# Segment 0 of a memory-recurrent attention during the weight loads, with V stores on two queues and part of chunk 1 projected early

## The chip, the core and the metric

One core of a Trainium2 chip runs the kernel. The metric is the time of one execution on the device in microseconds (us); for the kernel before it is the median of eight runs. A profile is one execution taken by the hardware profiler; its span runs from the first to the last instruction.

The engines are PE (TensorE: matmuls, with weight loads shown as PEld), DVE (VectorE), ACT (ScalarE), POOL (GpSimd) and SP (SyncE, which only issues DMAs here). Sixteen DMA engines move data for queues that SP, ACT and POOL feed.

## The reference, cut to what matters

```python
h  = x + A(layernorm(x), mem0, Wq, Wk, Wv, Wo)     # x: 2048 x 512
out = h + B(layernorm(h), w_in, w_sp, b_sp, w_out)

def A(x, mem, ...):                # 32 heads of 128, 64 segments of 32 rows, 8 memory rows
    for s in range(64):
        hs = concat([mem, x[32*s:32*s+32]])           # 40 rows
        q, k, v = hs @ Wq, hs @ Wk, hs @ Wv           # 512 -> 32 heads x 128
        p = softmax(mask(q @ k.T * scale))
        o = (p @ v) @ Wo                              # back to 512
        mem = o[:8]; outs.append(o[8:])               # the next segment needs this one's memory
def B(x, ...):                     # a gated MLP with a 2048 x 2048 mixing of the rows
    z = gelu(x @ w_in); z1, z2 = split(z); z2 = layernorm(z2)
    return (z1 * (w_sp @ z2 + b_sp)) @ w_out
```

Part A is a recurrence of 64 segments: the memory rows that a segment puts out go into the next one.

## The kernel before, in words

A small emitter records every operation in program order with the tiles that it reads and writes; each engine then executes its own operations in that order, with semaphore waits where another engine's result is needed (`Emitter.add`, L57). A DMA is an operation of the queue that issues it: SP for nearly all. DMAs take one of 40 semaphores in turn.

**Load phase.** SP loads two tiles of x, then Wq, Wk, Wv and Wo, each in four pieces of 1 MB (L287, L703). Of the 32 rows of a segment, the last 8 ("extra rows", the segment length less the memory rows gives 24 others) are projected to Q, K and V ahead of time, 16 segments (a *chunk*) at once: a tile hTe holds the 128 extra rows of a chunk, transposed. `qkx_mm` (L371) is one group of 16 matmuls, four heads of Q or K; `qkx_evac` (L383) moves it to QTx. `vx_mm` (L392) is one group for V; `vx_evac` (L401) moves it to one of two Vs buffers and a DMA stores that to vext_d in DRAM, from which `load_vx` (L412) fetches what a segment needs into Vx. In the load phase chunk 0 is done: 16 Q/K groups (L690) and 8 V groups (L705 to L708), whose stores are issued by ACT. `ln_inplace` (L331) normalises a tile of x (DVE and POOL in turn), `xT` (L342) transposes it on PE, `ring_copy` and `xe_copy` move it to hT (24 rows of each of four segments) and hTe (extra rows). `late_consts` (L303) makes masks and selectors on POOL.

**Segment loop** (L764). A segment does in order: Q and K for two halves of the heads (`QK`, L431; PE L437), eviction and transposition (`QK_evac`, ACT and DVE), scores (`S_half`), exp, V (`V_half`, L531), sums, reciprocal and normalisation of the softmax, p times v (`PV_half`, L548 and L554, the latter with Vx), eviction to cT, `Wo` (L581), eviction to part (one of eight slots), `mem_out` (L600 and L603), which writes the next segment's memory rows to hT. Between these PE gets other work by hand: `gx.pour(16)` (L819) puts one Q/K group of the next chunk ahead of `PV_half`; `gv.pour` puts the four pieces (four matmuls each) of a V group at L833 (one, ahead of Wo), L847 (two, after Wo) and L856 (one, after mem_out), in the segments whose index in the chunk is in VXS (L745). So chunk c is projected while chunk c-1 runs, and in segments 48 to 63 nothing is poured. Every fourth segment adds the four segments' results to x (`F_group`, `h_done`). Every second segment SP transposes a piece of w_sp by DMA (`wT_piece`, L778).

After segment 63 part B runs; it is not touched.

Of the kernel before, what the change touches and what calls it, by code (L numbers as in the profile page):

```python
# [33 lines left out]
class Emitter:  # L34
    ENGS = ("pe", "act", "dve", "pool", "sp")

    def __init__(self, n_dma_sems=16):
        self.ops = []
        self.by_eng = {e: [] for e in self.ENGS}
        self.last_w = {}  # L40
        self.readers = {}
        self.n_dma_sems = n_dma_sems
        self.dma_rr = 0
        self.dma_cnt = [0] * n_dma_sems
        self.dma_last = [None] * n_dma_sems
        self.const_tokens = set()
# [4 lines left out]
    def add(self, eng, fn, reads=(), writes=(), dma=False, after=()):  # L51
# [17 lines left out]
        if eng == "pool" and self.by_eng["pool"]:  # L69
            deps.add(self.by_eng["pool"][-1])  # L70
        if eng == "pe":
            deps = {d for d in deps if d.eng != "pe" or d.is_dma}
        if dma:
            j = self.dma_rr
            self.dma_rr = (self.dma_rr + 1) % self.n_dma_sems
            op.is_dma = True
            op.dma_sem = j
            self.dma_cnt[j] += 1
            op.dma_val = 16 * self.dma_cnt[j]
            if self.dma_last[j] is not None:  # L80
                deps.add(self.dma_last[j])
            self.dma_last[j] = op
# [9 lines left out]
        self.ops.append(op)  # L92
        op.pos = len(self.by_eng[eng])
# [67 lines left out]
def fast_path(nc, st, keep, A_x, A_mem0, A_Wq, A_Wk, A_Wv, A_Wo, A_seg_len, B_w_in, B_w_sp, B_b_sp, B_w_out, out):  # L161
# [15 lines left out]
    CK = 16  # L177
# [29 lines left out]
    hTe = sb("hTe", [128, 2, DC, 128], BF)  # L207
# [69 lines left out]
    def load_x(rb, j):  # L277
        sp(lambda e: e.dma_start(xn[:, j, :], xr[:, rb, :]), writes=[("xn", j)])

    def load_xe(ck, j):  # L280
        sp(lambda e: e.dma_start(xn[:, j, :], xe[CK * ck:CK * ck + CK, XM:SEG, :]), writes=[("xn", j)])
# [9 lines left out]
    load_xe(1, 1)  # L291
    for hq in range(4):
        load_w(0, hq)
    sp(lambda e: e.dma_start(m0[:], A_mem0[0]), writes=["m0"])
# [36 lines left out]
    def ln_inplace(j):  # L331
        dve(lambda e: e.bn_stats(out=st1[:, j, :], in_=xn[:, j, :]), reads=[("xn", j)], writes=[("st1", j)])
        dve(lambda e: e.bn_aggr(out=mv1[:, j, :], in_=st1[:, j, :]), reads=[("st1", j)], writes=[("mv1", j)])
        pool(lambda e: e.tensor_scalar(out=rs1[:, j:j + 1], in0=mv1[:, j, 1:2], scalar1=EPS, scalar2=None, op0=ALU.add),
             reads=[("mv1", j)], writes=[("rs1", j)])
        pool(lambda e: e.tensor_tensor(out=rs1[:, j:j + 1], in0=rs1[:, j:j + 1], in1=mhalf[:, 0:1], op=ALU.pow),
             reads=[("rs1", j), "mhalf"], writes=[("rs1", j)])
        dve(lambda e: e.tensor_scalar(out=xn[:, j, :], in0=xn[:, j, :], scalar1=mv1[:, j, 0:1], scalar2=rs1[:, j:j + 1],
                                      op0=ALU.subtract, op1=ALU.mult),
            reads=[("xn", j), ("mv1", j), ("rs1", j)], writes=[("xn", j)])  # L340

    def xT(j, bank):  # L342
        for dc in range(DC):
            pe(lambda e, dc=dc: e.transpose(out=psb[:, bank, dc * 128:(dc + 1) * 128], in_=xn[:, j, dc * 128:(dc + 1) * 128],
                                            identity=ident[:, :]),
               reads=[("xn", j), "ident"], writes=[PB(bank)])
# [10 lines left out]
    def xe_copy(ck, bank):  # L357
        src = psb[:, bank, 0:512].rearrange("p (dc c) -> p dc c", dc=DC)
        act(lambda e: e.activation(out=hTe[:, ck % 2, :, :], in_=src, func=ACT.Copy), reads=[PB(bank)], writes=[("hTe", ck % 2)])
# [10 lines left out]
    def qkx_mm(ck, i, bank, only_hh=None, only_dc=None):  # L370
        mi, h0 = i // 8, 4 * (i % 8)  # L371
        ws = (w_q, w_k)[mi]
        for hh in range(4):
            h = h0 + hh
            for dc in range(DC):
                if only_hh is not None and (hh, dc) != (only_hh, only_dc):
                    continue
                pe(lambda e, h=h, dc=dc, hh=hh: e.matmul(ps[:, bank, hh * 128:(hh + 1) * 128], lhsT=ws[:, dc, h * DH:(h + 1) * DH],  # L378
                                                         rhs=hTe[:, ck % 2, dc, :], start=(dc == 0), stop=(dc == DC - 1)),
                   reads=[("hTe", ck % 2), ("W", mi, h // 8)], writes=[PB(bank)])  # L380
# [10 lines left out]
    def vx_mm(ck, n, bank, only=None):  # L391
        for dc in range(DC):  # L392
            if only is not None and dc != only:
                continue
            for c in range(4):
                q = slice(32 * c, 32 * c + 32)
                pe(lambda e, dc=dc, c=c, q=q: e.matmul(ps[q, bank, :], lhsT=hTe[:, ck % 2, dc, q], rhs=w_v[:, dc, n * 512:(n + 1) * 512],  # L397
                                                       start=(dc == 0), stop=(dc == DC - 1), tile_position=(0, 32 * c)),
                   reads=[("hTe", ck % 2), ("W", 2, n // 2)], writes=[PB(bank)])

    def vx_evac(ck, n, bank, eng="act", queue="sp"):  # L401
        j = n % 2
        if eng == "act":
            act(lambda e: e.activation(out=Vs[:, j, :], in_=ps[:, bank, :], func=ACT.Copy), reads=[PB(bank)], writes=[("Vs", j)])
        else:
            dve(lambda e: e.tensor_copy(out=Vs[:, j, :], in_=ps[:, bank, :]), reads=[PB(bank)], writes=[("Vs", j)])
        b, c = n // 4, n % 4
        dst = vext_d[ck, 4 * c:4 * c + 4, :, b * DH:(b + 1) * DH].rearrange("g t e -> t g e")
        em.add(queue, lambda e: e.dma_start(dst, Vs[:, j, :].rearrange("p (g e) -> p g e", g=4)), dma=True, reads=[("Vs", j)],
               writes=[("vext", ck, n)])  # L410

    def load_vx(s):  # L412
        i = s % CK
        sp(lambda e: e.dma_start(Vx[:, s % NVX, :, :], vext_d[s // CK, :, 8 * i:8 * i + 8, :]),
           reads=[("vext", s // CK, n) for n in range(8)], writes=[("Vx", s % NVX)])
# [259 lines left out]
    for j in range(2):  # L675
        ln_inplace(j)
        xT(j, 6 + j)
        xe_copy(j, 6 + j)
    load_x(0, 0)
    load_x(1, 1)  # L680
    for hq in range(4):
        load_w(1, hq)
    late_consts()
    ebank = (0, 1, 2, 3)

    def start_group(cnt, mm, ev, *a):
        bk = ebank[cnt % 4]
        mm(*a, bk)
        ev(*a, bk, "act" if cnt % 2 == 0 else "dve")

    for i in range(16):
        start_group(i, qkx_mm, qkx_evac, 0, i)
        if i == 7:
            for j in range(2):
                ln_inplace(j)
                xT(j, 6 + j)
                ring_copy(j, 6 + j)
            mem0_transpose(5)
# [6 lines left out]
    for n in range(8):  # L705
        bk = ebank[n % 4]
        vx_mm(0, n, bk)
        vx_evac(0, n, bk, "act" if n % 2 == 0 else "dve", "act")  # L708
    for s in range(2):
        load_vx(s)  # L710
# [20 lines left out]
    gx, gv = Gap(), Gap()  # L731

    def qkx_atoms(ck, i):
        mms = [lambda ck=ck, i=i, hh=hh, dc=dc: qkx_mm(ck, i, XB, hh, dc) for hh in range(4) for dc in range(DC)]
        f = lambda: qkx_evac(ck, i, XB, "dve")
        f.eng = "dve"
        gx.add(XB, mms, f)

    def vx_atoms(ck, n):
        mms = [lambda ck=ck, n=n, dc=dc: vx_mm(ck, n, VXB, dc) for dc in range(DC)]  # L740
        f = lambda: vx_evac(ck, n, VXB, "act")
        f.eng = "act"
        gv.add(VXB, mms, f)

    VXS = (0, 1, 4, 5, 7, 8, 9, 12)  # L745
# [18 lines left out]
    for s in range(NSEG):  # L764
        j4 = s % 4
        rb = s // 4
        ck, i16 = s // CK + 1, s % CK
        if ck < NCK:
            if i16 == 0:
                for n in range(8):  # L770
                    vx_atoms(ck, n)
            qkx_atoms(ck, i16)
# [4 lines left out]
        if s % 2 == 0 and s // 2 < NWT:  # L777
# [3 lines left out]
        if i16 == 11 and 2 <= ck + 1 < NCK:  # L781
            load_xe(ck + 1, 1)
# [6 lines left out]
        if s == NSEG - 1:  # L789
            load_wT(0, [lastop["q"]])  # L790
        S_half(s, 0)
        sm_exp(0)
        V_half(s, 0)
# [11 lines left out]
        sm_rcp(0)  # L805
        V_half(s, 1, (0, 1, 2))
# [12 lines left out]
        ev = gx.pour(16)  # L819
# [12 lines left out]
        vx = i16 in VXS  # L832
        late = gv.pour(vx)  # L833
# [11 lines left out]
        if i16 == 12 and 2 <= ck + 1 < NCK:  # L845
            ln_inplace(1)
        late += gv.pour(2 * vx)  # L847
# [3 lines left out]
        if i16 == 13 and 2 <= ck + 1 < NCK:  # L851
            xT(1, XB)
            late.append(lambda: xe_copy(ck + 1, XB))
        if s + 1 < NSEG:
            mem_out(s)
        late += gv.pour(vx)  # L856
# [15 lines left out]
    assert not gx.atoms and not gv.atoms  # L872
# [922 lines left out]
```

## Time and profile before

| what | value |
|---|---|
| median of 8 runs | 941.97 us (939.97 to 944.39) |
| the profiled execution's own time | 940.55 us |
| its span | 938.7 us |
| PE busy | 881.3 us (94%) |
| ACT, DVE, POOL busy | 478.5, 445.3, 109.0 us |
| HBM read, written | 39.46 MB, 18.61 MB |
| first Q/K group (L378) on PE | 8.44 us |
| first V group (L397) on PE | 33.37 us |
| segment 0's Q and K (L437) | 49.92 us |
| segment 1's Q and K | 64.05 us |
| segment 48's Q and K | 582.49 us |

In the views a row begins with the line of the kernel, the engine and the operation; then the tile written and the tiles read, their shapes, and how many. A bracket at the end of a timeline row says how long the engine sat idle before it and what ended that. In the windows each row is a stretch of time: its length, the busy time of PE, PEld, DVE, ACT and POOL with the number of instructions, the granted clock of PE as a share of full speed, the busy share of the DMA engines and GB/s. In the chain of waits a row is a start, a duration and what the end of the program can be followed back to.

### The profile page before, as it was taken

To read this page: it belongs to the slowest core of one execution; us is meant where nothing else is said; L and a number is where in the kernel's file an instruction comes from. 1 tells how busy PE (TensorE), PEld (TensorE's weight loads), DVE (VectorE), ACT (ScalarE), POOL (GpSimd) and SP (SyncE) were. 2 spreads that over 40 slices of the span, in tenths; PEclk is the share of its full clock that TensorE was granted. 3 is DMA by queue.
4 is the path that set the end of the run, shared out by engine and by line. 5 is a ranking of instruction groups with operands and counts; after the bars stand their busy time and mean duration, and the time that the engine had idled before them with its cause. 6 is when DMAs were issued, how large, how long until landed. Compare 5 with 4: busy or idle time off the path is not lost.

```text
span 938.7 us, 45489 instructions
## 1 busy us (share of the span) xinstructions
PE 881.3 (94%) x20973; PEld 492.1 (52%) x20973; DVE 445.3 (47%) x1029; ACT 478.5 (51%) x1158; POOL 109.0 (12%) x274
## 2 busy tenths in 40 slices
PE   4789999999999999999999999989989999989998
PEld 4545555555555556555555555444544444434443
DVE  3134445455555445554545555444434464453434
ACT  2156566666666666666666656565656565500000
POOL 5001011011111111111111011111101022200000
PEclk9889999999999999999999999999999999999999
DMA  9942012130222222121212130513112193021201
GB/s 332 377 121 68 17 37 66 48 82 21 62 55 57 46 63 46 46 59 39 60 37 66 42 82 13 123 29 79 48 42 58 33 293 116 1 90 37 93 17 36
DMA packets 103668, 71.29 MB, mean 76 GB/s; under 512 B 62248, under 2 KB 89008, under 8 KB 103472
## 3 DMA queue, kind: packets, MB, share of 16 engines
q1 hardware_dynamic: 99248, 67.27, 24.9%
q8 instruction: 166, 2.72, 1.3%
q10 hardware_dynamic: 4224, 1.05, 0.5%
q14 instruction: 30, 0.25, 0.1%
HBM read 39.46 MB, written 18.61 MB: 62 GB/s over the span
## 4 chain that ended last, share of the span: by engine, by line
PE 89%; ACT 3%; DMA 3%; DVE 2%; issue 1%; SPq 0%; POOL 0%; ACTq 0%; DVEq 0%; POOLq 0%
PE f_ps L437 24%; PE f_ps L581 12%; PE f_ps L531 11%; PE f_ps L938 10%; PE f_ps L378 6%; PE f_ps L625 4%; PE f_ps L900 3%; PE f_ps L548 3%; PE f_ps L931 2%; PE f_ps L1008 2%; PE f_ps L397 2%; PE f_ps L600 2%; DMA vext_d<-f_Vs 2%; PE f_ps L476 2%; PE f_ps L497 1%
## 5 line engine op out<-in xcount | busy, mean ns | idle before, releaser
L437 PE MATMUL f_ps<-f_arena,f_hT 128*32 128x512 bf16 x4096 | 235.7, 383 | 17.9 <-ACT f_hT L603 12.0
L444 ACT ACTIVATE f_Tst<-f_ps 128x512 bf16<-128x512 f32 x256 | 152.6, 597 | 103.1 <-PE f_ps L437 101.2
L437 PEld LDWEIGHTS f_ps<-f_arena,f_hT 128*32 128x32 bf16 x4096 | 105.7, 97 | 127.4 <-ACT f_hT L603 24.0
L531 PE MATMUL f_ps<-f_arena,f_hT 128*32 128x512 bf16 x2048 | 140.2, 378 | 0.0
L450 DVE STREAM_TRANSPOSE f_QT<-f_Tst 128x256 uint32<-128x256 uint32 x128 | 57.0, 445 | 174.6 <-ACT f_Tst L444 174.6
L581 PE MATMUL f_ps<-f_arena,f_cT 128*32 128x384 bf16 (+1 forms) x4096 | 123.6, 273 | 1.6 <-ACT f_cT L567 1.5
L581 PEld LDWEIGHTS f_ps<-f_arena,f_cT 128*32 128x32 bf16 x4096 | 84.8, 97 | 55.4 <-ACT f_cT L567 26.4
L938 PE MATMUL f_ps<-f_arena 128*128 128x512 bf16 x448 | 101.3, 379 | 2.4 <-DVE f_arena L944 1.6
L593 ACT ACTIVATE f_part<-f_ps 128x384 bf16<-128x384 f32 (+1 forms) x128 | 46.4, 384 | 74.7 <-PE f_ps L581 74.7
L453 DVE STREAM_TRANSPOSE f_KT<-f_Tst 128x256 uint32<-128x256 uint32 x128 | 57.0, 445 | 52.7 <-ACT f_Tst L444 52.7
L460 POOL COPY f_QT<-f_arena 128x256 bf16<-128x256 bf16 x64 | 30.7, 480 | 392.2 <-PE f_ps L482 392.2
L569 DVE TENSOR_SCALAR f_cT<-f_ps 128x320 bf16<-128x320 f32 x128 | 56.9, 486 | 38.2 <-PE f_ps L554 38.2
L938 PEld LDWEIGHTS f_ps<-f_arena 128*128 128x128 bf16 x448 | 43.5, 98 | 55.9 <-DVE f_arena L944 2.6
L378 PE MATMUL f_ps<-f_hTe,f_arena 128*128 128x128 bf16 x1024 | 69.3, 225 | 0.7 <-DMA f_arena<-in_A_Wq_dram 0.7
L378 PEld LDWEIGHTS f_ps<-f_hTe,f_arena 128*128 128x128 bf16 x1024 | 60.7, 101 | 12.3 <-issue 12.3
L567 ACT ACTIVATE f_cT<-f_ps 128x320 bf16<-128x320 f32 x128 | 49.0, 435 | 34.2 <-PE f_ps L554 34.2
L517 DVE SCALAR_TENSOR_TENSOR f_E_sb<-f_R_sb,f_E_sb 128x160 bf16<-128x160 f32 x128 | 41.7, 326 | 46.5 <-ACT f_R_sb L513 46.5
L509 ACT ACTIVATE f_R_sb<-f_ps 128x160 f32<-128x160 f32 x128 | 39.0, 304 | 35.8 <-PE f_ps L502 35.8
L531 PEld LDWEIGHTS f_ps<-f_arena,f_hT 128*32 128x32 bf16 x2048 | 44.6, 95 | 21.0
L589 POOL COPY f_cTx<-f_cT 128x256 bf16<-128x256 bf16 x64 | 26.2, 410 | 196.6 <-DVE f_cT L569 196.6
L944 DVE TENSOR_TENSOR f_arena<-f_ps,f_arena 128x512 f32<-128x512 f32 x28 | 19.3, 691 | 57.8 <-PE f_ps L938 57.8
L389 DVE CAST f_arena<-f_ps 128x512 bf16<-128x512 f32 x56 | 38.2, 683 | 16.0 <-PE f_ps L378 16.0
(95 smaller groups left out, 1086.9 us busy)
## 6 DMA issues: line engine op xcount, KB each, us to landing
wT_d<-f_wst SPq DMA_DIRECT2D x32, 256.0 KB, 2.5
f_arena<-wT_d SPq DMA_DIRECT2D x32, 256.0 KB, 4.3
f_arena<-in_A_Wq_dram SPq DMA_DIRECT2D x4, 1024.0 KB, 8.8
f_arena<-in_A_Wk_dram SPq DMA_DIRECT2D x4, 1024.0 KB, 14.0
f_arena<-in_A_Wv_dram SPq DMA_DIRECT2D x4, 1024.0 KB, 14.5
f_arena<-in_A_Wo_dram SPq DMA_DIRECT2D x4, 1024.0 KB, 15.3
f_Vx<-vext_d SPq DMA_DIRECT2D x64, 64.0 KB, 2.9
vext_d<-f_Vs SPq DMA_DIRECT2D x24, 128.0 KB, 2.1
```

Of the source, the lines that this page charges most:

```text
L378: pe(lambda e, h=h, dc=dc, hh=hh: e.matmul(ps[:, bank, hh * 128:(hh + 1) * 128], lhsT=ws[:, dc, h * DH:(h + 1) * DH], rhs=hTe[:, ck % 2, d ...
L437: pe(lambda e, dc=dc, c=c, rhs=rhs: e.matmul(ps[32 * c:32 * c + 32, bank, :], lhsT=hT[:, sl, dc, :], rhs=rhs, start=(dc == 0), stop=(dc == ...
L444: act(lambda e: e.activation(out=Tst[:, tb, :].rearrange("p (hp i r) -> p hp i r", i=32, r=2), in_=ps[:, bank, :].rearrange("p (hp r i) -> ...
L450: dve(lambda e: e.transpose(out=dst, in_=src), reads=[("T", tb)], writes=[("QT", b)])
L453: dve(lambda e: e.transpose(out=dst, in_=src), reads=[("T", tb)], writes=[("KT", b)])
L517: dve(lambda e: e.scalar_tensor_tensor(out=E_sb[:, b, 0:160], in0=R_sb[:, b, :], scalar=RK, in1=E_sb[:, b, 0:160], op0=ALU.mult, op1=ALU.m ...
L531: pe(lambda e, dc=dc, c=c, c0=c0: e.matmul(ps[32 * c:32 * c + 32, bank, :], lhsT=hT[:, sl, dc, :], rhs=w_v[:, dc, c0:c0 + 512], start=(dc ...
L567: act(lambda e: e.activation(out=dst, in_=src, func=ACT.Copy, scale=UNSC), reads=[PB(PVB[c])], writes=[("cT", c)])
L569: dve(lambda e: e.tensor_scalar(out=dst, in0=src, scalar1=UNSC, scalar2=None, op0=ALU.mult), reads=[PB(PVB[c])], writes=[("cT", c)])
L581: pe(lambda e, h=h, g=g, i=i, b=b, c=c: e.matmul(ps[32 * g:32 * g + 32, bank, 0:d1 - d0], lhsT=cTh[:, i, 8:40], rhs=w_o[:, h, d0:d1], star ...
L593: act(lambda e: e.activation(out=part[:, s % 8, d0:d1], in_=ps[:, bank, 0:d1 - d0], func=ACT.Copy), reads=[PB(bank)], writes=[("part", s % ...
L938: pe(lambda e: e.matmul(ps[:, bank, 0:TB], lhsT=z2[:, sc, fb * 128:(fb + 1) * 128], rhs=wTb[tb % 2][:, :, sc, :], start=(sc == 0), stop=(s ...
```

## The change

Eight things are done. (1) x tiles of the start are loaded into free slots of `part` as well, all ahead of Wk, and hTe has three buffers, so the extra rows of chunk 2 are prepared at the start; those of chunk 3 are loaded at segment 4. (2) The groups of the load phase rotate over banks 2 to 5, so that segment 0's Q and K (banks 0, 1, 6, 7) can follow directly. (3) The first four Q/K groups of chunk 1 are put between those of chunk 0. (4) The eight V groups of chunk 0 move into segment 0, two, two and four at a time. (5) They are evicted to the eight slots of `part`, so no eviction waits for an earlier store; the stores alternate between ACT's and POOL's queue; the first two Vx loads are issued by POOL; POOL's DMAs have four semaphores of their own and POOL's compute no longer takes a POOL DMA as its predecessor. (6) Q/K groups 4 to 7 of chunk 1 follow in segment 0. (7) In the segments the slot ahead of `PV_half` takes whole groups from one list: the 8 V groups of chunk 1, its remaining 8 Q/K groups, then those of chunks 2 and 3. The V pieces of chunks 2 and 3 are poured one after mem_out in every segment and one more after Wo in two of four. (8) `wT_piece` moves from even to odd segments, `late_consts` behind the four norms of the load phase.

```diff
@@ Emitter.add
-        if eng == "pool" and self.by_eng["pool"]:
-            deps.add(self.by_eng["pool"][-1])
+        if eng == "pool" and not dma:
+            if self.last_pool is not None:
+                deps.add(self.last_pool)
...
         if dma:
-            j = self.dma_rr
-            self.dma_rr = (self.dma_rr + 1) % self.n_dma_sems
+            if eng == "pool":
+                self.sw_rr = (self.sw_rr + 1) % 4
+                j = self.n_dma_sems - 4 + self.sw_rr
+            else:
+                j = self.dma_rr
+                self.dma_rr = (self.dma_rr + 1) % (self.n_dma_sems - 4)
...
-    hTe = sb("hTe", [128, 2, DC, 128], BF)
+    hTe = sb("hTe", [128, 3, DC, 128], BF)
...
+    def xbuf(j):
+        return (xn[:, j, :], [("xn", j)]) if j < 2 else (part[:, j, :], [("part", j, 0), ("part", j, 1)])
...
     load_xe(0, 0)
-    load_xe(1, 1)
     for hq in range(4):
         load_w(0, hq)
+    load_xe(1, 1)
+    load_x(0, 4)
+    load_x(1, 5)
+    load_xe(2, 6)
...
     def vx_evac(ck, n, bank, eng="act", queue="sp"):
-        j = n % 2
+        if ck == 0:
+            t, tok = part[:, n, :], [("part", n, 0), ("part", n, 1)]
+        else:
+            j = vcnt[0] % 2
+            vcnt[0] += 1
+            t, tok = Vs[:, j, :], [("Vs", j)]
...
-    def load_vx(s):
+    def load_vx(s, queue="sp"):
...
-    for j in range(2):
-        ln_inplace(j)
-        xT(j, 6 + j)
-        xe_copy(j, 6 + j)
-    load_x(0, 0)
-    load_x(1, 1)
+    ln_inplace(0)
+    xT(0, 6)
+    xe_copy(0, 6)
     for hq in range(4):
         load_w(1, hq)
-    late_consts()
-    ebank = (0, 1, 2, 3)
+    ebank = (2, 3, 4, 5)
...
+        if mm is vx_mm:
+            ev(*a, bk, eng, {"act": "act", "dve": "pool"}[eng])
...
     for i in range(16):
-        start_group(i, qkx_mm, qkx_evac, 0, i)
+        start_x(0, i)
+        if i == 5:
+            ln_inplace(1)
+            ln_inplace(4)
         if i == 7:
-            for j in range(2):
-                ln_inplace(j)
-                xT(j, 6 + j)
-                ring_copy(j, 6 + j)
-            mem0_transpose(5)
+            ln_inplace(5)
+            ln_inplace(6)
+            late_consts()
...
+        if i >= 9 and i % 2 == 1:
+            start_x(1, i // 2 - 4)
...
-    for n in range(8):
-        bk = ebank[n % 4]
-        vx_mm(0, n, bk)
-        vx_evac(0, n, bk, "act" if n % 2 == 0 else "dve", "act")
-    for s in range(2):
-        load_vx(s)
...
+    for n in range(8):
+        vx_group(1, n)
+    for ck, i0 in ((1, 8), (2, 0), (3, 0)):
+        for i in range(i0, 16):
+            qkx_group(ck, i)
+    for ck in (2, 3):
+        for n in range(8):
+            vx_atoms(ck, n)
...
-        if s % 2 == 0 and s // 2 < NWT:
+        if s % 2 == 1 and s // 2 < NWT:
             wT_piece(s // 2)
...
+        if s == 0:
+            for n in range(2):
+                start_v(n)
         S_half(s, 0)
         sm_exp(0)
+        if s == 0:
+            for n in range(2, 4):
+                start_v(n)
         V_half(s, 0)
...
+        if s == 0:
+            for n in range(4, 8):
+                start_v(n)
         V_half(s, 1, (0, 1, 2))
...
-        ev = gx.pour(16)
+        if s == 0:
+            for j in range(2):
+                load_vx(j, "pool")
+            for i in range(4, 8):
+                start_x(1, i)
+        ev = [gx.pop(0)()] if gx else []
         PV_half(s, 0)
...
-        late += gv.pour(2 * vx)
+        if j4 < 2:
+            late += gv.pour(1)
...
-        late += gv.pour(vx)
+        late += gv.pour(1)
```

## The prediction, made before the changed kernel ran

> **What bounds the kernel now.** I read the page first: PE is busy for 94% of a span of 938.7 us and holds 89% of the chain that ended last. That share is an average over stages, so I went to the two stages that the change touches: the loading of the weights, and the 64 segments.
>
> The start, by windows of 1 us (the last two columns are the share of the DMA engines and GB/s, before them the granted clock), then the chain of waits and the timeline over 0 to 65 us:
>
> ```profile
> 35.00:36.00 1.00, 1.00 (x28) 0.45 (x21) 0.66 (x1) 0.07 (x1) 0.00 (x0) 1.00 1.06 391
> 40.00:41.00 1.00, 0.00 (x0) 0.00 (x0) 0.00 (x0) 0.00 (x0) 0.00 (x0) 1.00 1.14 360
> 49.00:50.00 1.00, 0.08 (x4) 0.08 (x8) 0.00 (x0) 0.60 (x1) 0.00 (x0) 0.50 1.11 358
> 50.00:51.00 1.00, 1.00 (x12) 0.37 (x16) 0.00 (x0) 0.00 (x0) 0.00 (x0) 0.50 0.48 149
> ```
> ```profile
> 36.06 7.17 DMA vext_d<-f_Vs
> ...
> 44.05 6.98 DMA vext_d<-f_Vs
> ...
> 51.84 1.96 DMA vext_d<-f_Vs
> ```
> ```profile
> 42.28 3.46 PE L397 MATMUL f_ps<-f_arena,f_hTe 128*32 128x512 bf16 x32 [3.54 <-ACT f_Vs L404]
> 49.92 6.55 PE L437 MATMUL f_ps<-f_arena,f_hT 128*32 128x512 bf16 x64 [4.18 <-ACT f_Vs L404]
> 56.58 1.71 SPq L414 DMA_DIRECT2D f_Vx<-vext_d  x2
> 60.15 0.27 PE L548 MATMUL f_ps<-f_E_sb,f_V_sb 32*128 32x40 bf16 x16
> 61.24 1.93 PE L581 MATMUL f_ps<-f_arena,f_cT 128*32 128x384 bf16 x64 [0.20 <-ACT f_cT L567]
> 64.05 3.64 PE L437 MATMUL f_ps<-f_arena,f_hT 128*32 128x512 bf16 x64
> ```
>
> The reader is to see three things. The DMA engines are full until 50.0 us, when the last weight (Wo) is in. Beside them the eight stores of V go out in pairs, because there are two Vs buffers: one pair takes 7.17 and 6.98 us, the last only 1.96 us when the loads are over. Everything behind them waits: segment 0's Q and K begin at 49.92 and segment 1's at 64.05. And after an idle PE (3.54 us, 4.18 us) the granted clock is 0.50: the 64 matmuls of L437 take 6.55 us there and 3.64 us at full clock.
>
> Then the segments, by the starts of L437:
>
> ```profile
> 141.99 3.64 PE L437 MATMUL f_ps<-f_arena,f_hT 128*32 128x512 bf16 x64
> 152.98 3.64 PE L437 MATMUL f_ps<-f_arena,f_hT 128*32 128x512 bf16 x64
> 582.49 3.64 PE L437 MATMUL f_ps<-f_arena,f_hT 128*32 128x512 bf16 x64 [0.32 <-ACT f_hT L603]
> 593.40 3.64 PE L437 MATMUL f_ps<-f_arena,f_hT 128*32 128x512 bf16 x64 [0.30 <-ACT f_hT L603]
> ```
>
> From segment 48 on nothing of the next chunk is poured in, and a segment takes 10.91 us (582.49 to 593.40): a chain of dependent steps, not PE work. With one group of L378 it takes 10.95, with four V pieces more 10.99, and only segments 7, 23 and 39 (V pieces beside the F group) take 11.42. So nearly all projection in the segments is hidden already. Segments 1 to 47 take 582.49 - 64.05 = 518.44 us, 5.7 us over 47 floors of 10.91: that is all that moving work out of them can bring.
>
> **The change, part by part.**
>
> *Loads.* The windows up to 36 us sum to 12.63 MB; 16 weight pieces and four x tiles are 17.30 MB; the remaining 4.67 MB at 388 GB/s (the windows from 20 to 36) would end at 48.0. It was 50.0, so four stores cost 2.0 us. The packet row of the ACT queue gives the same from another side:
>
> ```profile
> q10 hardware_dynamic: 4224, 1.05, 7.3%
> ```
>
> 7.3% of 64 us over eight stores is 0.58 us each. The change adds one x tile (0.34 us) to the stream and brings all eight stores into it: 48.3 + 8 x 0.5 to 0.58 = 52.3 to 53.0. I take 52.6. The x tiles are loaded with no wait for a free buffer; SP was never short of loads, so that alone is worth 0.
>
> *PE before the stores.* V moves behind QK of segment 0. DVE is first held by four norms of about 2.2 us (18.62 to 20.93 was one) from about 16.5, so its evictions 9 and 11 come near 26.4 and PE continues there: seven projection groups of 1.0, transposes 1.0, QK 3.64, eight V groups of 0.9 (x16 at 57 ns), segment 0's own V 1.5 and scores 0.5. That is 47 us for the last V group; its data are there near 38.6. The constants on POOL (7.59 to 18.87, 11.3 us) now start at about 25.3, after the norms, and end near 36.6; the scores need them at about 40. That cover is 3 us; when it is gone PE waits for POOL.
>
> *The stores.* They wait for no buffer any more (eight slots of `part`) and go out between about 39.6 and 48, four on ACT and four on POOL. They can't all be out before the stream as a whole has moved them, so the last lies between 50 (the stores get more than their share) and 53. I take 52.0. A store alone lands 1.96 us after issue, of which 0.5 is moving, so add 1.4: 53.4. Then POOL issues the load of Vx: 2.6 us from issue to landing (the two Vx loads of before, on SP). PV of segment 0 starts at 56.0.
>
> No row shows a DMA issued by POOL. Its issue lies between ACT's 0.37 us and SP's slowest 1.29 us for a plain tile; queued on POOL behind it are the qx copy for segment 1 and the cTx copy, needed 10 us later, so they are covered. I take the low end, as ACT's row is of the same transfer. The edits to the emitter (own semaphores for POOL's DMAs, POOL's compute no longer waiting for its last DMA) add no instruction; their worth is 0, hidden by POOL's idle time (109 us busy of 939). The Trainium skill ("DMA: Bandwidth & Descriptors", Specifications) has a first byte after about 1 us on this path against 0.6 us on the others; no row here shows it, and by it PV would be at 56.4, an estimate.
>
> *The rule against it.* In the rows a pair on one queue took 7.17 us while the loads kept 360 GB/s: it was the turn among queues that held the stores, not the issue. The same page (Rules for kernel authors) says that spreading DMAs over issuing engines brings no bandwidth, since all run on the same 16 engines. By the rule the end of the stream stays at 52.6, as in my sum; by the other reading two queues get two turns, the stores are out by 50, and rival A holds.
>
> *From PV to segment 1.* In before 60.15 to 64.05 is 3.9 us at full clock. PE has done its extra four groups and the first V group of chunk 1 by about 52.5 and idles some 3.5 us, as before the 0.50 rows. At that clock Wo alone takes 1.93 us more; I add 2.0. Segment 1 starts at 56.0 + 5.9 = 61.9 instead of 64.05: **-2.15 us**.
>
> *The segments.* 48 pops remain; eight are V groups (0.9 for 1.0, at most 0.04 off each), which replaces the eight Q/K groups done in the load phase. V pieces are now two, two, one, one per four segments: segments 7, 23 and 39 lose 0.46 each, 1.4 in all. The other V segments (0.04 above the rest) keep half: -0.4. Against it a piece behind mem_out in more segments, hidden under the hT eviction (0.21) as now, 0 to +0.8. Bounds: -1.4 - 0.8 - 0.3 (the pops) = -2.5, and -1.4 + 0.8 = -0.6; I take **-1.8**. Those eight V groups are evicted by DVE instead of ACT; the slot had a DVE eviction of the same size already (683 ns, L389), so 0, and were that cover gone, 0.69 us in eight segments. Their stores go through SP ahead of the Vx load for two segments later, so a late store has some 10 us. The rows of chunk 2 are taken at the start and those of chunk 3 at segment 4, under other work both times; 0. The transposing pieces of w_sp move to odd segments: DMA only, no row waits for it; 0. In the second half nothing changes.
>
> Sum: -2.15 - 1.8 = -4.0 on the profiled execution's own 940.55: 936.6. The median of the runs is 941.97, 1.4 higher, so 938.0.
>
> **The rivals.**
>
> A, the stores are out early and PE stays warm: last store at 50, PV at 54.0, +3.9 = 57.9, -6.1, with -1.9: **934.0**. For: the second queue, idle gap near 3 us. Against: the V groups end late on PE.
>
> B, the front is only moved: the last store waits out the stream and half clock lasts into QK (6.55 for 3.64), PV 57, +7.2: 64.2, +0.1; with the low end of the segments (-0.6): **941.5**. For: 0.50 after both idles. The new wait is Vx in place of Vs.
>
> C, slower: POOL's DMAs are dear. From about 41 four stores and then the Vx load are issued in order by POOL; with t us each, PV is near 41 + 5t + 2 + 2 and it decides above t = 2.2; at t = 4, PV is 65, segment 1 at 71 (+7), less 1.8: **947**. From t = 3.4 it is slower. Nothing in the rows prices it (ACT 0.37, SP 1.29).
>
> **How the numbers follow.** Main case 0.48 (own range 935.5 to 940), A 0.22, B 0.18, C 0.12. The range leaves out C and the far end of A: 931.5 to 942.5. A measurement of this kernel can tell about 0.2% (1.9 us) from no change; faster by more is the main case, but for its end, and A: 0.68; within it B and the rest: 0.20; slower C: 0.12.
>
> **What would show it.** L437 of segment 1 near 62; DMA full to 52.6; L548 of segment 0 waiting for the Vx load, not for Wo; clock 0.50 there; segments 7, 23, 39 at 10.96. Wrong if POOL's DMA rows are over 2 us, if the scores of segment 0 wait for POOL, or if segments 0 to 7 exceed 11.0 because the V group in the slot is dearer than L378.

## The result, and the profile after

| what | before | after |
|---|---|---|
| median of the runs | 941.67 us (40 runs, 938.68 to 944.75) | 937.22 us (15 runs, 935.34 to 939.17) |
| ratio after/before, 95% interval | | 0.9952 (0.9941 to 0.9963) |
| the profiled execution's own time, its span | 940.55, 938.7 | 937.59, 935.9 |
| segment 0's Q and K start | 49.92 | 35.21 |
| segment 1's Q and K start | 64.05 | 62.79 |
| segments 1 to 47 (starts of segments 1 to 48) | 518.44 | 515.65 |
| segments 48 to 62 | 163.71 | 163.66 |
| from segment 63's Q and K to the end of the span | 192.5 | 193.8 |

The change is faster by 4.5 us at the median (941.67 x 0.0048; interval 3.5 to 5.6). The profiled pair differs by 3.0 us. Its rows add up: -1.26 up to segment 1, -2.79 over segments 1 to 47, -0.05 over 48 to 62, +1.2 after that, which is -2.9 of span, and 0.1 lies around the span.

The last row is no effect of the change: part B is the same code in all thirteen profiles of this study and took 192.5 to 195.2 us, with the 192.5 of before as the lowest. Part of that scatter is the clock: four profiles (act_only, warm3, v_mix_sp, b_slots) have 3.4 us at 0.50 in part B, between 827 and 838 us, and they took 194.5 to 195.2, the nine others 192.5 to 193.9. Without that row the profiled pair differs by 4.1 us, close to the medians. A single profiled total is therefore good to about 2 us here, and what follows compares starts of segments.

**Up to segment 1.** The windows of after (length, busy PE, PEld, DVE, ACT, POOL, then granted clock, DMA share, GB/s):

```profile
51.00:52.00 1.00, 1.00 (x22) 1.00 (x20) 0.16 (x1) 0.54 (x1) 0.00 (x0) 1.00 1.08 356
57.00:58.00 1.00, 0.42 (x24) 0.29 (x24) 0.11 (x1) 0.18 (x1) 0.00 (x0) 0.50 0.10 29
```

The DMA engines are full to about 52.6, where they had been full to 50.0 (in windows of 0.2 us the share is 0.98 or more up to there, then 0.59): all eight stores now leave inside the stream of weights. PE works at full clock beside them, then the clock falls to 0.50. The chain of waits of after says on what:

```profile
46.98 7.54 DMA vext_d<-f_part
...
55.06 2.26 DMA f_Vx<-vext_d
...
58.31 3.60 PE f_ps L608 x63
```

And the timeline of after, PE's rows and POOL's load:

```profile
49.84 3.75 PE L398 MATMUL f_ps<-f_hTe,f_arena 128*128 128x128 bf16 x64 [1.04 <-ACT f_V_sb L565]
55.06 1.09 POOL L441 DMA_DIRECT2D f_Vx<-vext_d  x2 [4.94 <-DMA vext_d<-f_part]
57.36 0.24 PE L581 MATMUL f_ps<-f_E_sb,f_Vx 32*128 32x64 bf16 x4 [2.59 <-DMA f_Vx<-vext_d]
62.79 3.94 PE L464 MATMUL f_ps<-f_arena,f_hT 128*32 128x512 bf16 x64
```

Before, PE waited 3.54 and 4.18 us for Vs buffers. Those waits are gone, and 14.7 us of lead (49.92 to 35.21) has become 1.26: PE fills the time with projection work until 54.8 and then waits 2.59 us for Vx, because a store of V that left at 46.98 takes 7.54 us to land. Wo (L608) then runs at half clock, 3.60 us, where segments 1 to 62 have 1.93. The clock stays at 0.50 until 63.5, into segment 1's Q and K, so segment 1 takes 11.22 us where segments 2 to 5 take 10.91. The prediction named more than 11.0 there as a sign of a dear V group; it is the clock, for c1_late and warm3 have the same V group, full clock there, and 10.91.

**The segments.** What cost 11.42 us in segments 7, 23 and 39 is seen on PE between Wo and the memory rows. Segment 7 of before (F group L610, its scatter L635, V pieces L397, memory rows L600, then the next segment), and segment 23 of after (L637, L662, L627, V piece L417):

```profile
140.51 0.39 PE L610 MATMUL f_ps<-f_part,f_F_sb 128*32 128x512 bf16 x4
140.72 0.39 PE L635 MATMUL f_ps<-f_partx,f_Sc 128*32 128x512 bf16 x4
140.94 0.60 PE L397 MATMUL f_ps<-f_arena,f_hTe 128*32 128x512 bf16 x8
141.37 0.33 PE L600 MATMUL f_ps<-f_G_sb,f_part 128*32 128x8 bf16 x16
```
```profile
314.24 0.39 PE L637 MATMUL f_ps<-f_part,f_F_sb 128*32 128x512 bf16 x4
314.45 0.39 PE L662 MATMUL f_ps<-f_partx,f_Sc 128*32 128x512 bf16 x4
314.67 0.31 PE L627 MATMUL f_ps<-f_G_sb,f_part 128*32 128x8 bf16 x16
314.83 0.39 PE L417 MATMUL f_ps<-f_arena,f_hTe 128*32 128x512 bf16 x4
```

PE's order is fixed, so the memory rows, on which the next segment hangs, stand behind whatever is put ahead of them; their input, the eviction of part on ACT (L593), is done at 141.01. From the F group to the memory rows it is 0.86 us before (140.51 to 141.37) and 0.43 after; segments 7, 23 and 39 go from 11.43, 11.42, 11.41 to 10.99, 10.96, 10.97.

### The profile page after: what moved, and what is told of

Read it like the earlier page. It is cut to its first block, busy times and chain, and to the rows that moved or that the text cites. A ratio compares the mean times of both kernels' runs of the same rounds, so it can differ in the third digit from the quotient of the medians.

```text
span 935.9 us, 45484 instructions
## 1 busy us (share of the span) xinstructions
PE 887.2 (95%) x20973; PEld 488.1 (52%) x20973; DVE 447.4 (48%) x1033; ACT 475.8 (51%) x1154; POOL 113.1 (12%) x280
## 3 DMA queue, kind: packets, MB, share of 16 engines
q1 hardware_dynamic: 98960, 67.14, 25.9%
## 4 chain that ended last, share of the span: by engine, by line
PE 90%; ACT 3%; DMA 2%; issue 2%; DVE 1%; SPq 1%; POOL 0%; POOLq 0%
PE f_ps L464 25%; PE f_ps L608 13%; PE f_ps L558 11%; PE f_ps L1003 10%; PE f_ps L398 6%; PE f_ps L652 4%; PE f_ps L965 3%; PE f_ps L575 3%; PE f_ps L996 3%; PE f_ps L1073 2%; PE f_ps L627 2%; PE f_ps L417 2%; PE f_ps L503 2%; ACT f_hT L630 1%; PE f_ps L524 1%
## 5 line engine op out<-in xcount | busy, mean ns | idle before, releaser
L608 PE MATMUL f_ps<-f_arena,f_cT 128*32 128x384 bf16 (+1 forms) x4096 | 125.4, 275 | 2.7 <-ACT f_cT L594 2.1
L608 PEld LDWEIGHTS f_ps<-f_arena,f_cT 128*32 128x32 bf16 x4096 | 84.8, 97 | 61.5 <-ACT f_cT L594 31.4
L575 PE MATMUL f_ps<-f_E_sb,f_V_sb 32*128 32x40 bf16 x2048 | 36.3, 178 | 10.4 <-DVE f_E_sb L549 8.9
```

The source lines that it names most:

```text
L575: pe(lambda e, q=q, c=c, g=g, c0=c0: e.matmul(ps[:, PVB[c], c0:c0 + 40], lhsT=V_sb[q, b, g * 128:(g + 1) * 128], rhs=E_sb[q, b, g * 40:(g ...
L608: pe(lambda e, h=h, g=g, i=i, b=b, c=c: e.matmul(ps[32 * g:32 * g + 32, bank, 0:d1 - d0], lhsT=cTh[:, i, 8:40], rhs=w_o[:, h, d0:d1], star ...
```

## The experiments

Each kernel is after (or before, where said) with the edit shown; c1_late_sp and v_mix_sp are c1_late and v_mix with one edit more. Times to segment 1 and over segments 1 to 47 are from its profiled execution; the ratio is to before, with its 95% interval.

| kernel | median us | ratio (interval) | segment 1 at | segments 1 to 47 |
|---|---|---|---|---|
| after | 937.22 | 0.9952 (0.9941 to 0.9963) | 62.79 | 515.65 |
| act_only | 936.67 | 0.9957 (0.9938 to 0.9975) | 63.38 | 515.47 |
| two_bufs | 943.33 | 1.0020 (1.0006 to 1.0033) | 68.59 | 515.63 |
| c1_late | 934.46 | 0.9927 (0.9903 to 0.9950) | 60.44 | 515.34 |
| c1_late_sp | 933.91 | 0.9919 (0.9892 to 0.9946) | 58.24 | 515.46 |
| warm3 | 935.59 | 0.9934 (0.9912 to 0.9956) | 60.88 | 515.33 |
| v_early | 936.60 | 0.9947 (0.9926 to 0.9968) | 60.90 | 515.45 |
| v_mix | 933.14 | 0.9918 (0.9887 to 0.9948) | 57.97 | 515.36 |
| v_mix_sp | 933.16 | 0.9927 (0.9907 to 0.9946) | 57.95 | 515.75 |
| vxs_back | 938.91 | 0.9985 (0.9971 to 0.9999) | 61.78 | 516.71 |
| b_slots (of before) | 939.99 | 0.9976 (0.9961 to 0.9991) | 62.60 | 517.46 |
| b_spread (of before) | 940.99 | 1.0001 (0.9986 to 1.0016) | 62.83 | 517.20 |

The table also shows the spread of a profiled execution. vxs_back has after's code up to segment 1 (but for two V pieces in segment 0: from Wo's end to Q and K is 0.88 us in after, 0.87 without them) and reaches it 1.0 us sooner; b_spread has before's and reaches it 1.2 us sooner. The pair of these two gives -1.05 for the front where the pair of after and before gave -1.26.

This spread has a cause that the profiles show. In before the clock is 0.50 from 21.5 to 28.3 us, in b_spread from 22.8 to 26.2 only, and from there on b_spread is 1.1 us ahead. In after it is 0.50 from 22.5 to 25.9, in vxs_back not at all there, and segment 0's Q and K start 1.9 us sooner (33.35); most of that is lost again in the wait for Vx, and ahead of segment 1 the half clock lasts 6.8 us in after and 3.4 in vxs_back. So a difference of about 1 us in the start of segment 1 between two kernels can be the clock alone, and vxs_back is a second sample of after's front.

### act_only: one queue instead of two

```diff
-            ev(*a, bk, eng, {"act": "act", "dve": "pool"}[eng])
+            ev(*a, bk, eng, "act")
...
-                load_vx(j, "pool")
+                load_vx(j)
```

> All eight V stores of chunk 0 are issued by ACT and the first two Vx loads by SP; POOL issues no DMA. In the changed kernel the last store landed at 55.0, PV of segment 0 got its Vx at 57.36 and segment 1 began at 62.79. Theory (the DMA engines' total work sets the last store, not the number of queues): last store at 54 to 55.5, segment 1 at 62 to 63.5, time 937.2 within 1. Rival (a second queue gives the stores a second turn beside the loads): last store 3 us later, near 58, segment 1 near 65.8, time 940.

The last store landed at 54.90; with two queues it was 54.52 (54.06 in vxs_back). The second queue is worth 0.4 to 0.8 us at that place, where the rival had 3. What one queue does cost is ACT's time. The timeline of act_only, ACT's issues and PE:

```profile
44.19 3.12 ACTq L434 DMA_DIRECT2D vext_d<-f_part  x2
47.98 2.89 ACTq L434 DMA_DIRECT2D vext_d<-f_part  x2
52.13 6.52 PE L398 MATMUL f_ps<-f_hTe,f_arena 128*128 128x128 bf16 x64 [4.79 <-ACT f_V_sb L565]
```

ACT stood in the issue of two stores for 3.12 and 2.89 us, where a single one in after takes 0.37 (the first four stores of act_only also took 0.37 to 0.39 each, beside equally full DMA engines), and evicted segment 0's own V that much later. PE waited 4.79 us for it in place of 1.04, fell to half clock and came to p times v at 59.56 with Vx long there; Wo then ran at full clock (1.93). One wait replaces another and segment 1 starts 0.6 us later. At the median that is not to be seen (the intervals cover each other).

### two_bufs: the two Vs buffers again

```diff
-        if ck == 0:
-            t, tok = part[:, n, :], [("part", n, 0), ("part", n, 1)]
-        else:
+        if True:
             j = vcnt[0] % 2
```

> The changed kernel with its V stores of chunk 0 again from two buffers, so an eviction waits for the store two before; queues as in the changed kernel. Theory (waiting stores lose the time in which the loads still run): pairs land near 47, 53, 56 and 58, PV near 60.5, segment 1 near 66.5, time 941. Rival (PE reaches the V groups so late that the slots are worth nothing): segment 1 at 62.8 to 63.3, time 937.2 to 937.7.

```profile
48.21 0.60 ACT L427 ACTIVATE f_Vs<-f_ps 128x512 bf16<-128x512 f32 x1 [7.49 <-DMA vext_d<-f_Vs]
57.88 5.98 PE L398 MATMUL f_ps<-f_hTe,f_arena 128*128 128x128 bf16 x64 [3.12 <-ACT f_V_sb L563]
60.38 1.09 POOL L439 DMA_DIRECT2D f_Vx<-vext_d  x2 [1.43 <-DMA vext_d<-f_Vs]
```

The rows of two_bufs show the old wait in its new place: ACT waits 7.49 us for a buffer whose store is on its way, and the last load of Vx leaves at 60.38 (55.06 in after). Segment 1 starts 5.8 us later and the median is 6.1 us higher, slower than before. That is worse than the theory (66.5 and 941). The staging slots are what the whole gain up to segment 1 hangs on; moving V into segment 0 without them loses.

### c1_late: the four early groups of chunk 1 behind the stores

```diff
-        if i >= 9 and i % 2 == 1:
-            start_x(1, i // 2 - 4)
...
-            for i in range(4, 8):
+            for i in range(8):
                 start_x(1, i)
```

> The first four Q/K groups of chunk 1 leave the load phase proper and follow behind the V stores of segment 0, with the other four. Theory (the last V group on PE sets the last store, and an idle PE costs half clock): V groups 4 us earlier, last store landed near 53, Vx at 55.4, PE busy until then and at full clock, segment 1 near 59.3, time 933.7. Rival (the end of the DMA stream sets it, whatever PE does): last store still at 55, Vx at 57.4, only the clock is gained, segment 1 near 61.3, time 935.7.

```profile
43.99 8.55 DMA vext_d<-f_part
53.08 3.62 DMA f_Vx<-vext_d
```

In the chain of c1_late the last store leaves at 43.99 instead of 46.98 and lands 2 us earlier. Part 3 of the change, four groups of 1.0 us ahead of V, thus delayed what the front waits for; undone, segment 1 starts at 60.44 (-2.35) and the median falls by 2.8. PE ends its queue at 54.7 as in after, but Vx is there 0.6 us sooner: the idle time is 2.05 us instead of 2.59, and the clock stays at 1.00. The 2.35 us are these 0.6 and what half clock costs.

The result lies between the theory (59.3, 933.7) and the rival (61.3, 935.7): the stores landed early, as the theory had it, but the load of Vx then took 3.62 us. Against vxs_back, the other sample of after's front, the last store lands 1.5 us sooner (52.54 for 54.06), Vx reaches PE at the same time (56.74 for 56.78), and the 1.3 us at segment 1 are all clock. That the earlier stores also bring Vx sooner is shown by c1_late_sp and v_mix (54.54 and 54.27).

### warm3: three more groups in segment 0

```diff
-            for i in range(4, 8):
+            for i in range(4, 11):
                 start_x(1, i)
...
-    for ck, i0 in ((1, 8), (2, 0), (3, 0)):
+    for ck, i0 in ((1, 11), (2, 0), (3, 0)):
```

(Three segments then have no group in the slot, so that the order of the others stays.)

> The changed kernel with three more Q/K groups of chunk 1 in segment 0, ahead of PV (seven instead of four), taken from the later segments; nothing else moves. PE was idle from 54.8 to 57.36 there and ran Wo in 3.60 us. Theory (half clock after the idle time costs the front about 2 us): PV at 57.6, Wo in 1.93 us, segment 1 near 61.5, time 936. Rival (the clock is worth nothing there, other waits fill the time): segment 1 at 62.8 to 63.1, time 937.2 or more.

```profile
57.18 0.21 PE L581 MATMUL f_ps<-f_E_sb,f_Vx 32*128 32x64 bf16 x4 [0.69 <-DMA f_Vx<-vext_d]
58.08 1.93 PE L608 MATMUL f_ps<-f_arena,f_cT 128*32 128x384 bf16 x64 [0.56 <-ACT f_cT L594]
```

Vx arrives as in after (57.18 against 57.36), the idle time before it is 0.69, the clock is 1.00 throughout, and segment 1 starts at 60.88 instead of 62.79. Of the 1.9 us 0.2 is Vx and 1.7 the clock (Wo's 3.60 for 1.93); another 0.3 follows in segment 1.

How long PE idles does not decide by itself whether the clock falls. 2.59 us (after) and 2.63 us (b_slots) ahead of Vx were enough and 2.05 us (c1_late) was not, but in the load phase 3.51 us in v_early and 3.33 us in vxs_back left the clock at 1.00. In all thirteen profiles the clock changes only at multiples of 3.41 us from one another, and what goes with a fall is how busy PE was in the stretch of 3.41 us that ends there. The stretch ahead of after's fall, then the two over which v_early's 3.51 us are spread (length, busy PE, and the clock third from the end):

```profile
53.22:56.63 3.41, 1.55 (x39) 0.70 (x36) 0.69 (x1) 0.11 (x1) 1.09 (x2) 1.00 0.18 53
15.66:19.07 3.41, 1.60 (x29) 1.43 (x26) 2.15 (x6) 0.60 (x1) 0.90 (x3) 1.00 1.06 369
19.07:22.49 3.42, 1.72 (x31) 1.75 (x32) 1.79 (x4) 0.63 (x2) 1.30 (x4) 1.00 1.05 388
```

Every such stretch at full clock with PE busy for up to 0.40 of it was followed by half clock, none with 0.47 or more was; of four between 0.41 and 0.46 only after's (1.55 of 3.41 us) was. c1_late has 1.79 us busy in the stretch with most of its 2.05 us of idle time (52.90 to 56.32). By these rows the same idle time is dear or free by where it falls among these stretches, which differs from one execution to the next.

The Trainium skill ("TensorE: Matmul & The Clock Gate", What's actually happening) says that the clock is halved after at least one idle window of about 3.4 us. These rows agree with the length and not with the idleness: PE was busy for 1.55 of the 3.41 us ahead of after's fall.

### v_early and v_mix: V groups ahead of segment 0's Q and K

```diff
+        if s == 0:
+            for n in range(8):
+                start_v(n)
+                if n in (1, 3, 5):
+                    start_x(1, n // 2)
         for b in range(2):
             for mi in range(2):
                 QK(s, b, mi)
...
-            for i in range(4, 8):
+            for i in range(3, 8):
                 start_x(1, i)
```

(v_mix; the early groups of chunk 1 and the other V groups are taken out as in c1_late. v_early is the same with all eight chunk-1 groups behind the stores.)

> All eight V groups of chunk 0 stand ahead of segment 0's Q and K, as Wv lands, and all eight Q/K groups of chunk 1 behind the stores. Theory: V groups from about 32 to 40, stores out by 51, Vx near 53.5, then Wo sets the end: segment 1 near 58, time 932.4. Rival (the end of the DMA stream sets the last store): last store near 54, Vx near 56.6, segment 1 near 60.5, time 935.

> V groups of chunk 0 ahead of segment 0's Q and K as before in the early variant (there segment 1 began at 60.90 and PV waited for PE's own eight Q/K groups, not for Vx); three of those groups are put into PE's waits for Wv (0.77, 0.91 and 0.99 us), five stay behind the Vx loads. Theory (in the early variant PE's queue is the bound): PE done near 53.5, Vx landed by then, PV 53.5, segment 1 near 57.4, time 931.7. Rival (Wo's landing or Vx is the bound in any case): segment 1 not below 60, time 934.5 or more.

In v_early the last store has landed at 48.5, and now PE is late itself: three waits for Wv of 0.77 to 0.99 us ahead of Q and K, then nine groups in a row from 48.80 to 57.1, so that p times v never waits for Vx. Segment 1 starts at 60.90 and the median is 936.60: neither the theory (58, 932.4) nor the rival, whose last store would have landed near 54. v_mix puts three of these groups into the waits for Wv, and PE is ready 0.5 us before Vx. The chain of v_mix, then its Wo in the timeline:

```profile
42.54 7.14 DMA vext_d<-f_part
...
49.96 4.26 DMA f_Vx<-vext_d
```
```profile
55.16 1.93 PE L608 MATMUL f_ps<-f_arena,f_cT 128*32 128x384 bf16 x64 [0.56 <-ACT f_cT L594]
```

Segment 1 starts at 57.97, 4.8 us before after; the median is 933.14, 4.1 us lower. With v_mix_sp it has the lowest median of the kernels tried, though the intervals of c1_late and c1_late_sp cover theirs. Its interval and that of after overlap at their ends (0.9948 and 0.9941), but only one of the eight runs of v_mix and v_mix_sp (935.35) is above the fastest run of after (935.34). The DMA engines are still full to about 52.3: the stores only go through earlier in the same stream.

### c1_late_sp and v_mix_sp: the first loads of Vx on SP instead of POOL

```diff
-                load_vx(j, "pool")
+                load_vx(j)
```

> The variant with all of chunk 1's Q/K groups behind the V stores (segment 1 at 60.44, Vx 3.66 us after the last store had landed), with the two Vx loads issued by SP instead of POOL. Theory (POOL's issue made that load slow): Vx 2.6 us after the last store, near 55.7, segment 1 near 59.4, time 933.4. Rival (the load is slow beside other transfers, whoever issues it): segment 1 at 60.2 to 60.6, time 934.5.

> The kernel after with the V groups ahead of segment 0's Q and K, three Q/K groups of chunk 1 between them, five behind, and the two first Vx loads issued by SP instead of POOL. Theory (a POOL-issued load lands later than an SP-issued one): Vx lands about 1 us earlier (3.2 us from issue for 4.3), but PE's own queue of five groups ends near 54.5 to 55, so Wo moves only from 55.16 to about 54.6: segment 1 at 57.4 for 57.97, about 932.6 for the 933.1 of the same kernel with POOL. Rival (the landing is set by the full DMA engines, not by the issuer): Vx lands at the same 54.3, segment 1 at 57.9 to 58.0, no difference.

In c1_late_sp Vx landed 2.35 us after its issue, in c1_late 3.62, which looked like the price of POOL. v_mix_sp refutes that. Its chain has the load of Vx by SP:

```profile
49.93 4.28 DMA f_Vx<-vext_d
```

That is 4.28 us against 4.26 by POOL in v_mix, at the same moment and beside the same full DMA engines, and the two medians agree (933.16 and 933.14). POOL's own load in after took 2.26 us where the DMA engines were idle, and SP's in b_slots took 2.25 in the same state. The issuer does not set it. Why c1_late's took 3.62 with DMA shares of 0.24 to 0.41 from 53 to 55 us stays open; SP's second load in c1_late_sp, issued at 52.73, took 3.68.

### b_slots: eight slots in the kernel before, and nothing else

```diff
         j = n % 2
+        if ck == 0:
+            t, tok = part[:, n, :], [("part", n, 0), ("part", n, 1)]
+        else:
+            t, tok = Vs[:, j, :], [("Vs", j)]
...
```

> The kernel before with one part of the change: eight staging slots for the V stores of chunk 0, all still issued by ACT; V groups, segment 0 and everything else as before. Theory (the waiting stores are what held segment 0): V groups to about 40, Q and K of segment 0 at 40 to 42, last store landed near 53, Vx near 55.7, PE idle before it and so half clock, segment 1 near 61.6, time 939.3. Rival (the stores' wait was hidden behind the Wo load anyway): segment 1 near 64, time 941.7.

```profile
39.01 3.30 ACTq L413 DMA_DIRECT2D vext_d<-f_part  x2
42.98 3.80 ACTq L413 DMA_DIRECT2D vext_d<-f_part  x2
56.42 0.24 PE L558 MATMUL f_ps<-f_E_sb,f_Vx 32*128 32x64 bf16 x4 [2.63 <-DMA f_Vx<-vext_d]
```

The slots alone bring before to the same state as after: the last store waits out the stream, p times v waits 2.63 us for Vx, Wo runs at half clock (3.60). ACT's queue is again what holds ACT (3.30 and 3.80 us for two issues), and PE waits 2.45 us for ACT inside segment 0. Segment 1 starts at 62.60, 1.45 sooner than in before and 1.0 later than the theory; the median falls by 1.3 us (from the 941.30 of before in the same series). Taking segment 0 into the loads adds nothing up to segment 1 that can be told over this (62.79 and 61.78 in the two samples of after's front), since both end with the same wait; the rest of after's gain is in the segments. By the profiles these bring about 2 us; the medians of the two kernels leave 3, within their intervals.

### vxs_back and b_spread: where the V pieces lie

```diff
-        late = []
+        vx = s >= CK and s % CK in (0, 1, 4, 5, 7, 8, 9, 12)
+        late = gv.pour(vx)
         Wo((0, 2, 1, 3), OB, 0, OC)
...
-        if j4 < 2:
-            late += gv.pour(1)
+        late += gv.pour(2 * vx)
...
-        late += gv.pour(1)
+        late += gv.pour(vx)
```
```diff
-    VXS = (0, 1, 4, 5, 7, 8, 9, 12)
+    VXS = (0, 1, 4, 5, 8, 9, 12, 13)
```

(The first is vxs_back, of after; the second b_spread, of before.)

> The kernel after with the V pieces of chunks 2 and 3 poured as before: four of them in each of eight segments of a chunk, one ahead of Wo. Theory (the gain of the segments comes from V pieces that no longer lie beside the F group): segments 23 and 39 go from 10.96 back to 11.42, the other V segments from 10.95 to 10.99 and those without to 10.91 or 10.95; segments 1 to 48 take 0.9 to 1.5 us more than 515.65, about 516.9; median about 938.4. Rival (the gain comes from the eight Q/K groups that were moved out of the segments): segments 1 to 48 stay at 515.6.

> The kernel before with the V pieces of index 7 in the chunk moved to index 13, and nothing else. Theory: segments 7, 23 and 39 fall from 11.42 to 10.96, segments 13, 29 and 45 rise by 0.04: segments 1 to 48 take 1.3 us less than 518.44, 517.1; segment 1 stays at 64.05; median 940.3. Rival (the 11.42 belongs to the F group or to the segment's place, not to the V pieces): segments 7, 23, 39 stay at 11.4, 518.4, no change.

In vxs_back segments 23 and 39 are back at 11.42 and 11.47, the other V segments at 10.99, and segments 1 to 47 take 1.06 us more. The median is 1.7 higher. Segment 7 stays at 10.93, since chunk 1's V still goes as whole groups into the slot; by b_slots (11.42) that is another 0.5. So at least 1.5 of the 1.8 to 2.8 us of the segments lie in the place of the pieces. What the groups that were moved out are worth by themselves was not run; 0.3 us are left for them beside the 1.8.

b_spread gave the sum that was expected (517.20 for 517.1) for a reason that was not. Segments 7, 23 and 39 fell to 10.96 or 10.97, but segments 13 and 29 rose from 10.96 and 11.14 to 11.40, while 45 rose only to 10.99. The timeline of b_spread in segment 13:

```profile
204.56 0.60 PE L397 MATMUL f_ps<-f_arena,f_hTe 128*32 128x512 bf16 x8
205.10 0.40 PE L344 MATMUL f_ps<-f_ident,f_xn 128*128 128x128 bf16 x4
205.43 0.27 PE L600 MATMUL f_ps<-f_G_sb,f_part 128*32 128x8 bf16 x16
```

There the transposes of the next chunk's extra rows (L344, in segments 13 and 29 only) stand between Wo and the memory rows. It is not the F group that is dear beside V pieces; PE has room there for one thing of about 0.45 us (in segment 7 of before the eviction of part ends 0.50 us after PE starts what stands behind Wo), and the second one is paid in full: 0.43 us in segment 7, 0.44 here. Part 1 of the change, which takes chunk 2's rows at the start and chunk 3's at segment 4, takes the transposes out of that place. At the median nothing moved (1.0001), as the two new segments take most of it back.

## Why the prediction was right, and where two errors cancelled

The forecast was 938.0 with -2.15 up to segment 1 and -1.8 in the segments; measured were 937.22, -1.26 and -2.79. The sum (-4.0 against -4.05) is better than its terms, by luck: the front brought 0.9 less and the segments of this pair 1.0 more, and that excess is mostly a stall in one execution of before. The mechanism held: Vx in place of Vs as the last wait, half clock behind it, and the segments' place of the V pieces.

- *Loads' end* 52.6: right. The last V group at 47: 47.84. The scores at about 40 and no wait for the constants: 40.40, the constants done at 37.26. No wait of the stores for a buffer: right.
- *The last store* was to land at 53.4, with POOL's load of Vx at once behind it; it landed at 54.52 and the load left at 55.06. This is the term that was mis-sized, by 1.66: the step "a store alone lands 1.96 us after issue, of which 0.5 is moving, so add 1.4" treated it as alone (1.12), and the 0.54 from the landing to POOL's issue was put at nothing. In the runs the store that the front waits for leaves beside the loads and takes 7.1 to 9.9 us (7.14 in v_mix, 7.54 in after, 9.89 in b_slots).
- *Vx* 2.6 us: 2.30 from issue to PE. *PV to segment 1* 5.9: 5.43. So 1.66 - 0.30 - 0.47 = 0.89, the miss of the front. *Half clock* +2.0: right as a mechanism; warm3 measures it at 1.7 up to segment 1 and 0.3 in it. That it came at all was partly luck, since the idle time was 2.59 us and not the 3.5 of the prediction, and c1_late with 2.05 kept its clock.
- *The rule against it*: the number of queues changes little at the end of the stores (act_only 54.90, after 54.52). But the two queues are not alike: in after ACT's four stores landed 7.5 to 8.5 us after issue and POOL's 5.5 to 6.6, and in c1_late POOL's last left 1.2 us after ACT's last and landed 1.8 us before it. All eight on POOL was not run. The Trainium skill ("DMA: Bandwidth & Descriptors", Issuing engines are not separate DMA queues) adds that several issuers save only the time of issuing, usually small. Here that time is 2.4 and 2.15 us for two pairs on ACT (3.12 and 2.89 less twice 0.37), on the path to PE; but the wait for Vx takes its place.
- *The segments*: -1.4 for 7, 23 and 39 (measured 0.44 to 0.46 each, 1.34) was right. The other V segments lost all of their 0.04 (10.99 to 10.95), where the prediction let them keep half. The prediction named only 7, 23 and 39 as long, and so counted before's stalls in segments 5 and 44 as room that a change could win. The excess lies mostly in the execution of before that was profiled: its segment 5 took 11.64 with a stall of 0.55 that nothing in the profile explains, and segment 44 took 11.32. b_slots has the same segments and took 517.46, which leaves -1.8 for the change by after's 515.65, or -2.0 by 515.46, the median of the nine kernels here that have after's segments.
- *POOL's DMAs* at the low end: a store's issue took 0.75 to 1.01 us, two to three times the 0.37 taken, off the path. Rival C, which needed 2.2 us, falls. Rival A needed stores out by 50 and a warm PE; v_mix is that kernel, and its segment 1 at 57.97 is A's 57.9, but by an earlier place of V, not by the second queue. Of rival B the half clock that lasts into Q and K came true (to 63.5 in after), with segment 1 at 62.79 between its 64.2 and the 61.9 of the main case.

## What to carry to other kernels

Work moved ahead of a wait gains only up to the next thing that ends last: follow what the moved work feeds (here the store of V and its load back), and put the producers of that first, filler after them. When loads keep the DMA engines full, a store among them lands with the stream, so its place in the order of issue matters more than a second queue, which moved the last landing by less than 1 us here (three earlier places moved it by 1.5 to 6). In a recurrence, look at what stands on the in-order engine just ahead of the instruction that feeds the next step: a gap there hides one filler, and the second is paid in full, in each step that has both. Before a difference of 1 us between two profiles is put down to an edit, compare their granted clocks.

## What the runs showed of the hardware that was not expected

- Issuing a store on ACT's queue can hold ACT: in act_only and b_slots the first four stores took 0.37 to 0.42 us each and the next four 1.09 to 2.67, with the DMA engines full for all eight. It set in with the fifth store while none (b_slots, act_only) of the first four had landed; kernels with four stores on ACT never show it. That it is the number on the queue was not tested. POOL issued at most four stores, each in 0.75 to 1.01 us.
- The queue rows in the profile of after (packets, MB, share of 16 engines) show that the two paths cut the same stores differently. By their sizes q10 has ACT's four stores (0.52 MB), and q0 has POOL's four and the two loads of Vx (0.66 MB):

```profile
q10 hardware_dynamic: 2112, 0.52, 0.3%
q0 software_dynamic: 256, 0.66, 0.2%
```

- Half clock comes in stretches of 3.4, 6.8 or 10.2 us: 22.5 to 25.9 and 56.6 to 63.5 in after, 57.0 to 60.4 in vxs_back, 43.3 to 53.5 in b_spread. It ended after a stretch of 3.41 us in which PE was busy for about 0.84 or more. How long it is paid for, and in which work, follows from how busy PE is behind the idle time.
- The Trainium skill (same section of "TensorE: Matmul & The Clock Gate") has a free-running window of 3413 ns; the stretches are one, two and three of them, which agrees with these rows.
- Identical code varies from one execution to the next: part B by 2.7 us over thirteen profiles, and the start of segment 1 by 1.0 and 1.2 us in two pairs of kernels that are the same up to there. For the second, and part of the first, the clock is the reason that the profiles show.
